# Pooled attention and an MLP on one core: the second MLP product of blocks 4 to 8 by seven products of quarters, copies ahead of remainders, and new priorities

## The chip, the cores and the metric

The kernel runs on one core of one Trainium2 chip. The metric is the device time of one execution in microseconds (us); a run gives the time of several executions, and one execution is also recorded by the hardware profiler. The engines are named as in the profile: PE is TensorE (with PEld, its weight loads), DVE is VectorE, ACT is ScalarE, POOL is GpSimd, and SP is SyncE, which here only issues DMAs.

## The reference

```python
# q, k, v: (4, 8, 1152, 64) float32; w_in (512, 2048) and w_out (2048, 512) float64
q_pool = q.reshape(B, H, S // 2, 2, D).mean(axis=3)              # 576 queries per head
scores = np.matmul(q_pool, k.transpose(0, 1, 3, 2)) / np.sqrt(D)
scores = scores - np.max(scores, axis=-1, keepdims=True)
attn = np.exp(scores)
attn = attn / (np.sum(attn, axis=-1, keepdims=True) + 1e-09)
x = np.matmul(attn, v).transpose(0, 2, 1, 3).reshape(2304, 512)  # 4 batches of 576 tokens
h = x @ w_in
out = np.maximum(0.01 * h, h) @ w_out
```

There are 32 heads (4 batches of 8), each with 576 pooled queries and 1152 keys, and then a two-layer MLP on 2304 tokens.

## The kernel before

**Two pieces for one number.** A float32 operand is split into a high part, rounded to the fast matmul format (`F32R`), and a remainder, also in that format. A product is then three matmuls: high x high, high x remainder, remainder x high. The functions whose names end in `_hi` make the copies, those in `_lo` the remainders (value minus high part).

**Attention.** A head (`hd`) loads its keys and queries, adds pairs of queries (`q_sum`), transposes both on PE (`k_tr`, `q_tr`) into a PSUM bank, and splits them. The keys sit in the bank as two halves of 64 partitions; `k_hi` copies half 0 or 1 on ACT (64 x 512 elements), and `k_lo` subtracts on DVE. For the queries `q_hi` copies each half twice on ACT (64 x 288 elements), and `q_lo` makes the remainder on DVE. The two halves are interleaved in the same tile. Then follow the maxima of the scores (`qk` on PE, `vmax` on DVE), the scores again with the maximum taken off (`qkt`), the exponentials on ACT (`exp`), the sums on POOL (`esum`), the product with the values (`pv`), and the norm. The result goes to DRAM (`xd`), one tile per batch.

**Weights.** In the course of the attention `w_in` and `w_out` are loaded, turned from float64 into float32 and split. The pieces of `w_in` go to DRAM (`wd`) and come back for each block (`ws_load`, 16 tiles of 512 KB); those of `w_out` stay in SBUF (`wo[0..15]`, 128 rows of `w_out` each).

**MLP.** There are 9 blocks of 256 tokens (`i`). A block loads its input (`x_load`) into the only buffer of `xb`, splits it (`x_hi`, `x_lo`), and makes 16 row tiles (`f`) of the hidden layer with `l1`: 12 matmuls of 128 x 128 on 256 columns each. Two of them fill a PSUM bank; `post` applies the leaky ReLU on ACT, copies the high part on DVE or ACT, and makes the remainder on POOL, into a buffer `gg` that is kept until `l2` has read it. `l2` makes the output of 128 tokens (`j`) over 8 row tiles (`hf`), three matmuls of 512 columns per tile; `o_evac` copies the first half of the sum and adds the second on DVE, and `o_out` stores.

A block needs the batches that hold its tokens, so the first blocks run among the heads and the others behind them.

**The order.** Nothing is ordered by the engines themselves: each works through its queue, and waits in it. A planner in the kernel (`Scheduler`) writes the queues. It holds a list of steps, each with a priority, an estimated cost on the engines that could take it, the steps it depends on and the buffers it takes; it goes forward in its own estimated time, and of the steps that can start next takes the one with the smallest priority and the engine on which it would end first. `SHIFT` is a table of numbers added to the priorities, by kind of step and stage. SP's DMA issues are planned in the same way.

Of the kernel before, what the change touches and what calls it, by code (L numbers as in the profile page):

```python
# [9 lines left out]
F32 = mybir.dt.float32  # L10
# [28 lines left out]
PEEK = 0.0  # L39


SHIFT = {
    "esum": (-3.5, 24.75, 81.75, 0, 1.0),
    "exp": (36.25, 13.25, 0, -27.25, 12.75),
    "k_dup": (-5.25, -3.5, 4.5, 0, 8.5),
    "k_hi": (24.5, 16.0, -5.0, -100.0, -3.25),
    "k_lo": (-2.75, -27.0, 0.25, 51.5, -41.0),
    "k_tr": (38.25, 8.5, 23.25, -37.75, 20.0),
    "l1": (-4.75, -21.5),
    "l2": (-19.0, 1.25, 10.0),  # L50
    "load_k": (-73.75, -7.25, -10.0, 2.75, 15.25),
    "load_q": (-16.25, -4.0, 16.5, -12.0),
    "load_v": (0.5, 17.75, 10.0, 3.0, -8.0),
    "m_cp": (20.5, 1.0, 9.5, -10.5, 4.75),
    "m_dma": (-16.25, -44.0, -15.75, 30.25, 27.25),
    "m_side": (146.0, -20.25, 3.25, 12.25, 4.5),
    "m_tr": (-27.25, 0, -0.5, 0, 3.25),
    "norm": (-0.5, 25.0, 28.0, -2.25, 5.75),
    "o_evac": (0, -0.5, 8.0),
    "o_out": (-15.25, 1.0, 11.0),  # L60
    "post0": (9.0, -21.5),
    "post1": (-14.0, -12.5, -14.0),
# [12 lines left out]
    "r_mm": (0, -8.25, -7.75, -6.0, 18.0),
    "r_row": (51.0, -6.5, -20.5, -0.75),
    "r_wide": (1.0, 2.0, 35.5, 1.0, -7.75),
    "scale": (2.75, 0, -8.0, 0, -15.5),
    "vmax": (-16.75, -9.5, 13.0, -138.75, 36.5),
    "vneg": (1.0, 0, 2.0, 4.5),  # L80
    "w_f320": (-1.0, -3.0, -18.75, -38.5),
    "w_f321": (7.0, 127.25, 23.75, -39.75),
    "w_f322": (0, -8.0, 12.5, 44.25),
    "w_hi": (-7.5, 0, -1.25, 7.25),
    "w_lo": (119.75, -10.0, -9.0, -19.75),
    "w_load": (-15.0, 2.25, 18.75, 2.5),
# [30 lines left out]
class Scheduler:  # L117
# [76 lines left out]
    def start(self, s, e, at, pending):  # L194
# [20 lines left out]
        if s.lat:  # L215
            end = self.dma = max(self.dma, at + 1.2) + s.lat
            end += 1.2
# [21 lines left out]
def tile_pooled_attention_moe(  # L239
# [37 lines left out]
    def f32(t):  # L277
        return t.bitcast(F32)
# [31 lines left out]
    }  # L310

    banks = ps.tile([128, 8, 512], F32, name="banks")

    def new(tag, slot, dtype=None):
# [3 lines left out]
        _, shape, dt, _ = spec[tag]  # L318
# [6 lines left out]
        t = sb.tile(spec[own][1], dt, tag=f"{own}{i}", name=own)[:shape[0], :n]  # L325
# [7 lines left out]
    kbs = [sb.tile([128, S], F32R, name=f"kb{j}") for j in range(2)]  # L333
    qzs = sb.tile([128, 5 * 64], F32R, name="qzs")
    qls = [sb.tile([128, NQ * 128], F32R, name=f"ql{j}") for j in range(4)]
# [289 lines left out]
    xx, lps, gf, gg, po, acc = {}, {}, {}, {}, {}, {}  # L625

    def x_load(i, e, s):
        xx[i] = t = new("xb", s)
        n0 = 0
        while n0 < NB:  # L630
            b, o = divmod(i * NB + n0, SP)
# [5 lines left out]
    def x_hi(i, e):  # L637
        copy(e, xx[i][:, 0], f32(xx[i][:, 1]))
# [249 lines left out]
```

## Time and profile before

| what | value |
|---|---|
| median of 3 runs | 935.19 us (934.62 to 939.8) |
| the profiled execution, its own time | 937.15 us |
| its span, first to last instruction | 935.3 us |
| mean granted TensorE clock | 0.944 |
| PE busy | 897.0 us, 96% |
| DVE, ACT, POOL busy | 405.2, 416.1, 502.5 us |

A row of the groups by line reads: line, engine, operation, what is written <- what is read, shapes, count | busy time in total, mean ns of one | the engine's idle time just before, and what ended it. Busy times of PE come from modelled ends of pipelined matmuls; the distance between two starts is the better measure of what a matmul costs.

### The profile page before, as it was taken

The numbers are of one execution on the slowest core, as the hardware profiler recorded it, in microseconds if no ns is written. First come the engines' busy times: TensorE is split into PE (matmuls) and PEld (weight loads), VectorE is DVE, ScalarE is ACT, GpSimd is POOL, SyncE is SP. The second block draws the span as 40 slices with busy tenths as digits, with TensorE's granted clock in tenths as the row PEclk, the third lists the DMA queues.
The fourth block names the chain that finished last, engine by engine and source line by source line (L and its number), as shares of the span: only waits on it lengthen the run. The fifth ranks groups of instructions, "written<-read, shape, count | busy, mean of one in ns | idle before, by whom it ended". The sixth has DMA issues, their size and how long they took to land.

```text
span 935.3 us, 16304 instructions
## 1 busy us (share of the span) xinstructions
PE 897.0 (96%) x6048; PEld 724.4 (77%) x6048; DVE 405.2 (43%) x857; ACT 416.1 (44%) x842; POOL 502.5 (54%) x390
## 2 busy tenths in 40 slices
PE   5999999999899999999999999999999999999998
PEld 3776766677677777877777777787989898989986
DVE  6677887766665544554455544401101011111110
ACT  4677787666556554655665554433111111111110
POOL 2475778867668755766666666657222323232320
PEclk9799999999999999999999999999999999999999
DMA  6389877666656653542454444244658576666630
GB/s 169 100 241 268 246 214 209 182 185 208 204 160 164 194 155 101 162 139 74 144 160 122 123 119 123 66 124 130 226 173 271 189 241 218 204 206 202 221 127 23
DMA packets 113263, 158.66 MB, mean 170 GB/s; under 512 B 21633, under 2 KB 80161, under 8 KB 113185
## 3 DMA queue, kind: packets, MB, share of 16 engines
q1 hardware_dynamic: 113184, 157.64, 56.7%
q8 instruction: 47, 0.77, 0.4%
q14 instruction: 32, 0.25, 0.1%
HBM read 130.02 MB, written 17.90 MB: 158 GB/s over the span
## 4 chain that ended last, share of the span: by engine, by line
PE 73%; ACT 9%; DMA 6%; DVE 6%; issue 4%; SPq 1%; POOL 1%; ACTq 0%; DVEq 0%; POOLq 0%
PE banks L656 20%; PE banks L523 9%; PE banks L472 9%; PE banks L679 7%; PE banks L505 7%; PE banks L680 7%; PE banks L678 7%; PE banks L506 6%; ACT qh L435 3%; ACT ka L281 2%; DVE ka L386 2%; ACT e L510 2%; DMA rt<-rs 2%; DVE ql L439 1%; DMA ws<-wd 1%
## 5 line engine op out<-in xcount | busy, mean ns | idle before, releaser
L510 ACT ACTIVATE e<-banks 128x576 f32<-128x576 f32 x288 | 186.4, 651 | 195.5 <-PE banks L506 184.6
L515 POOL TENSOR_TENSOR sm<-sm,e 128x576 f32<-128x576 f32 x168 | 241.9, 1440 | 53.5 <-ACT e L510 47.5
L475 DVE TENSOR_REDUCE stat<-banks 128x1 f32<-128x384 f32 (+1 forms) x448 | 218.1, 535 | 84.7 <-PE banks L472 80.8
L656 PE MATMUL banks<-xb,ws 128*128 128x256 f32 x1728 | 235.1, 283 | 2.8 <-DMA ws<-wd 1.7
L656 PEld LDWEIGHTS banks<-xb,ws 128*128 128x128 f32 x1728 | 225.0, 189 | 10.3 <-DMA ws<-wd 1.9
L505 PE MATMUL banks<-qh,ka 128*128 128x288 f32 x576 | 170.4, 311 | 6.4 <-ACT e L510 5.9
L506 PE MATMUL banks<-ql,kb 128*128 128x288 f32 x576 | 161.9, 296 | 0.0
L523 PE MATMUL banks<-e,vv 128*64 128x288 f32 x1152 | 159.3, 424 | 0.0
L505 PEld LDWEIGHTS banks<-qh,ka 128*128 128x128 f32 x576 | 109.3, 190 | 33.2 <-ACT e L510 15.1
L472 PE MATMUL banks<-ka,qh 128*128 128x384 f32 x384 | 119.8, 373 | 15.2 <-DVE stat L475 7.0
L664 ACT ACTIVATE g<-banks 128x512 f32<-128x512 f32 x72 | 43.1, 599 | 192.0 <-PE banks L656 191.4
L523 PEld LDWEIGHTS banks<-e,vv 128*64 128x64 f32 x1152 | 78.3, 139 | 64.3 <-issue 16.2
L669 POOL TENSOR_TENSOR gg<-g,gg 128x512 fp32r<-128x512 f32 x50 | 64.4, 1289 | 88.4 <-DVE gg L281 87.3
L506 PEld LDWEIGHTS banks<-ql,kb 128*128 128x128 f32 x576 | 109.4, 190 | 2.4 <-DMA ql<-ms 0.3
L472 PEld LDWEIGHTS banks<-ka,qh 128*128 128x128 f32 x384 | 68.6, 194 | 34.5 <-DVE stat L475 16.9
L515 POOL TENSOR_TENSOR sm<-e 128x576 f32<-128x576 f32 x32 | 46.9, 1465 | 90.0 <-ACT e L510 90.0
L678 PE MATMUL banks<-wo,gg 128*128 128x512 f32 x200 | 79.5, 398 | 0.0
L679 PE MATMUL banks<-wo,gg 128*128 128x512 f32 x200 | 78.9, 395 | 0.0
L680 PE MATMUL banks<-wo,gg 128*128 128x512 f32 x200 | 78.7, 394 | 0.0
L669 POOL TENSOR_TENSOR ka<-g,ka 128x512 fp32r<-128x512 f32 x22 | 28.4, 1291 | 81.5 <-DVE ka L281 81.5
L281 DVE CAST gg<-g 128x512 fp32r<-128x512 f32 x32 | 15.9, 497 | 123.9 <-ACT g L664 123.9
L439 DVE SCALAR_TENSOR_TENSOR ql<-banks,qh 64x288 fp32r<-64x288 f32 x64 | 29.1, 454 | 83.5 <-ACT qh L435 83.1
(66 smaller groups left out, 946.1 us busy)
## 6 DMA issues: line engine op xcount, KB each, us to landing
ws<-wd SPq DMA_DIRECT2D x144, 512.0 KB, 4.6
kn<-in_k_dram SPq DMA_DIRECT2D x32, 288.0 KB, 5.0
qn<-in_q_dram SPq DMA_DIRECT2D x32, 288.0 KB, 4.1
vv<-in_v_dram SPq DMA_DIRECT2D x32, 288.0 KB, 4.7
kb<-ka SPq DMA_DIRECT2D x64, 128.0 KB, 2.9
raw<-in_moe_w_in_dram SPq DMA_DIRECT2D x16, 512.0 KB, 4.5
wd<-ws SPq DMA_DIRECT2D x16, 512.0 KB, 5.8
raw<-in_moe_w_out_dram SPq DMA_DIRECT2D x16, 512.0 KB, 5.5
```

The source lines that it names most:

```text
L472: nc.tensor.matmul(p, lhsT=lhsT, rhs=ka[hd][:, k0:k0 + w], start=(j == 0), stop=(j == 128 // n - 1))
L475: nc.vector.tensor_reduce(out=mx[hd][:, i, c:c + 1], in_=mps.pop((hd, i, c)), axis=AX.X, op=ALU.max)
L505: nc.tensor.matmul(p[:, hf, :HW], lhsT=ka[hd][:, ks], rhs=qh[hd][:, c], start=True, stop=False)
L506: nc.tensor.matmul(p[:, hf, :HW], lhsT=kb[hd][:, ks], rhs=ql[hd][:, c], start=False, stop=True)
L510: nc.scalar.activation(out=ex[hd, t], in_=sps.pop((hd, t))[:, :, :HW], func=AF.Exp)
L515: ENG[e].tensor_tensor(out=sm[hd], in0=ex[hd, 0] if t == 1 else sm[hd], in1=ex[hd, t], op=ALU.add)
L523: nc.tensor.matmul(p[64 * hf:64 * hf + 64, :HW], lhsT=vv[hd][:, t, :], rhs=ex[hd, t][:, hf], start=(t == 0), stop=(t == KT - 1),)
L656: nc.tensor.matmul(p, lhsT=wst[i, f][:, a, c, :], rhs=xx[i][:, x, c, :], start=(n == 0), stop=(n == 3 * KC - 1))
L669: ENG[e].tensor_tensor(out=t[:, 1], in0=gf.pop((i, fp)), in1=f32(t[:, 0]), op=ALU.subtract)
L678: nc.tensor.matmul(p, lhsT=gh, rhs=wo[f][:, 0], start=(f == hf * FH), stop=False)
L679: nc.tensor.matmul(p, lhsT=gh, rhs=wo[f][:, 1], start=False, stop=False)
L680: nc.tensor.matmul(p, lhsT=gl, rhs=wo[f][:, 0], start=False, stop=(f == hf * FH + FH - 1))
```

## The change

In blocks 0 to 3 (`i < FAST`) the MLP stays as it is. In blocks 4 to 8:

- The second product is taken as a product of 2 x 2 quarters: the tokens in two halves of 128, the hidden rows in two halves (row tile `p` and row tile `p + 8`), and the output columns in two halves of 256. In place of eight products of quarters there are seven, of sums and differences of quarters (Winograd's form), each again as three matmuls.
- The sums of the quarters of `w_out` are made once, for each of 8 pairs of row tiles: `w_sum`, then `w_top` (high part, on ACT) and `w_rest` (remainder). One of the four sums overwrites columns of `wo[p]`, so it waits for block 3's use of them. The buffers are those of the attention, after its last head.
- The hidden layer comes in another order (tiles `p + 8` and `p` together); `g_act` applies the leaky ReLU, `g_mix` makes four sums and differences of 128 columns, `g_hi` and `g_lo` the two pieces of all seven.
- `l2s` runs the seven products for one `p`: 21 matmuls of 256 columns into seven halves of four PSUM banks. For the last `p` it goes bank by bank. `o_mix` adds the seven results on DVE (one copy, seven additions), and `o_mix_out` stores.
- `x_load` gets a second buffer, from two buffers of the attention.

In all heads `k_lo` of either half now comes after `k_hi` of both halves, and `q_lo` after all four `q_hi`. The planner's estimate for DMAs changes (300 KB per us in place of 250, and started 0.45 us behind the issue), and the table `SHIFT` is new throughout.

```diff
+FAST = 4
+DEEP = 4
+LAG = 3.5
 SHIFT = {
-    "esum": (-3.5, 24.75, 81.75, 0, 1.0),
-    "exp": (36.25, 13.25, 0, -27.25, 12.75),
+    "esum": (-3.5, 20.75, 83.5, -27.75, -12.25),
+    "exp": (27.75, 25.75, -8.25, -9, 17.25),
...
-            end = self.dma = max(self.dma, at + 1.2) + s.lat
+            end = self.dma = max(self.dma, end + 0.45) + s.lat
...
-    tags["ml"] = [(early, 0, slots("bank", (6,), (3,))), (tail, 0, slots("bank", (0,), (1,), (2,), (3,), (4,), (7,)))]
-    tags["gg"].append((tail, 0, slots("ka", *[(i,) for i in range(spec["ka"][0])])))
+    tags["ml"] = [(early, 0, slots("bank", (6,), (3,))), (tail, 0, slots("bank", (0,), (1,), (2,), (3,), (4,), (5,), (7,)))]
+    end = NHD - 1
+    tags["gg"].append((("k_tr", end, 0), 0, slots("ka", (0,), (1,))))
+    tags["gg"].append((("k_dup", end), 0, slots("kb", (0,))))
+    tags["xb"].append((("k_tr", end, 0), 0, slots("ka", (2, 3))))
+    tags["wf"] = [(("k_tr", end, 0), 0, slots("ka", (0,))), (("k_dup", end), 0, slots("kb", (0,)))]
...
+    S1, S2, S3, S4, A12, A22, A11, A21 = range(8)
+    PRODUCTS = ((0, 0, A11), (0, 1, A12), (1, 0, S2), (1, 1, S1), (2, 0, S3), (2, 1, A22), (3, 0, S4))
+    def w_sum(p, part, e, i=None):
...
+        tt = ENG[e].tensor_tensor
+        if part == 0:
+            for n, a, b in ((2, b22, b12), (0, b12, b11)):
+                tt(out=t[:, n:n + 2], in0=a, in1=b, op=ALU.subtract)
+                tt(out=t[:, n], in0=t[:, n], in1=t[:, n + 1], op=ALU.add)
+        else:
+            for n, a, b, op in ((1, b22, 0, ALU.subtract), (3, b21, 1, ALU.subtract)):
+                tt(out=t[:, n], in0=a[:, 0], in1=t[:, b], op=op)
+                tt(out=t[:, n], in0=t[:, n], in1=a[:, 1], op=ALU.add)
...
+    def w_rest(p, n, e):
+        t = wt2[p, n]
+        ENG[e].tensor_tensor(out=t[:, 1], in0=wf[p][:, n], in1=f32(t[:, 0]), op=ALU.subtract)
+    def g_act(i, p, e, s):
+        fs_[i, p] = new("gf", s, F32)
+        src = lps.pop((i, p)).rearrange("p y n -> p (y n)")
+        dst = fs_[i, p][:, A12:].rearrange("p a n -> p (a n)")
+        nc.scalar.activation(out=dst, in_=src, func=AF.Prelu, alpha=0.01)
+    def g_mix(i, p, e):
+        t = fs_[i, p]
+        for o, a, b, op in ((S1, A21, A22, ALU.add), (S3, A11, A21, ALU.subtract), (S2, S1, A11, ALU.subtract), (S4, A12, S2, ALU.subtract)):
+            ENG[e].tensor_tensor(out=t[:, o], in0=t[:, a], in1=t[:, b], op=op)
+    def g_hi(i, p, e, s):
+        gh[i, p] = new("gs", s)
+        copy(e, gh[i, p].rearrange("p a n -> p (a n)"), fs_[i, p][:, :7].rearrange("p a n -> p (a n)"))
+    def g_lo(i, p, e, s):
+        gl[i, p] = new("gs", s)
+        ENG[e].tensor_tensor(out=gl[i, p], in0=fs_.pop((i, p))[:, :7], in1=f32(gh[i, p]), op=ALU.subtract)
+    def l2s(i, p, b, e, *got):
...
+        ws = (b11, b21, t2, t1, t3, t4, b22)
+        for (bank, half, a), w in zip(PRODUCTS, ws):
+            if b is not None and bank != b:
+                continue
+            o = pk[i, bank][:, 256 * half:256 * half + 256]
+            for n, (g, x) in enumerate(((gh, 0), (gh, 1), (gl, 0))):
+                nc.tensor.matmul(
+                    o, lhsT=g[i, p][:, a], rhs=w[:, x], start=(p == 0 and n == 0 and half == 0),
...
-                step(k_lo, hd, x, prio=pr + 0.1 * g, eng={"DVE": dve(n, psum=True)}, deps=[("k_hi", hd, x)])
+                step(k_lo, hd, x, prio=pr + 0.1 * g, eng={"DVE": dve(n, psum=True)}, deps=[("k_hi", hd, x), None if g else ("k_hi", hd, 1)])
...
-            step(q_lo, hd, x, prio=pr + 0.5, eng={"DVE": dve(HW, psum=True)}, deps=[("q_hi", hd, x, x)])
+            step(q_lo, hd, x, prio=pr + 0.5, eng={"DVE": dve(HW, psum=True)}, deps=[("q_hi", hd, 1, y) for y in range(2)])
...
+    for p in range(FH):
+        pr = 500 + p
+        last = [("l2s", NBLK - 1, p, 3 if p == FH - 1 else None)]
+        pools = {"POOL": 2 * (gp(512) + gp(256)), "DVE": 2 * (dve(512) + dve(256))}
+        step(w_sum, p, 0, prio=pr, eng=pools, lock=True, deps=[("w_lo", NF + p), ("w_lo", NF + FH + p)], takes=[("wf", [("w_rest", p, n) for n in range(4)])])
+        step(w_sum, p, 1, prio=pr, eng={"POOL": 4 * gp(256), "DVE": 4 * dve(256)}, lock=True, deps=[("w_sum", p, 0)])
+        for n in range(4):
+            deps = [("w_sum", p, n % 2)] + ([("w_sum", p, 1)] + [("l2", FAST - 1, 0, 1, x) for x in (p,)] if n == 0 else [])
+            takes = [("w2" if p == 0 and n == 1 else "w1", last)] if n and not (p == 0 and n == 2) else []
+            step(w_top, p, n, prio=pr, eng={"ACT": act(256)}, deps=deps + ([("w_top", 0, 1)] if p == 0 and n == 2 else []), takes=takes)
+            step(w_rest, p, n, prio=pr, eng={"POOL": gp(256), "DVE": dve(256)}, lock=True, deps=[("w_top", p, n)])
...
+                last = [("l2s", i, fp, x) for x in (range(4) if fp == FH - 1 else (None,))]
+                step(g_act, i, fp, prio=POST, eng={"ACT": act(512, True)}, deps=[("l1", i, f, 2)], takes=[("gg", [("g_lo", i, fp)], 2)])
+                step(g_mix, i, fp, prio=POST, eng={"DVE": 4 * dve(128), "POOL": 4 * gp(128)}, lock=True, deps=[("g_act", i, fp)])
+                step(g_hi, i, fp, prio=POST, eng={"ACT": act(7 * 128)}, deps=[("g_mix", i, fp)], takes=[("gg", last, 1)])
+                step(g_lo, i, fp, prio=POST, eng={"POOL": gp(7 * 128), "DVE": dve(7 * 128)}, lock=True, deps=[("g_hi", i, fp)], takes=[("gg", last)])
```

## Rows read from the trace of the kernel before

**Rows 1.** The page: span, and busy time of PE.

```profile
span 935.3 us, 16304 instructions
PE 897.0 (96%) x6048; PEld 724.4 (77%) x6048; DVE 405.2 (43%) x857; ACT 416.1 (44%) x842; POOL 502.5 (54%) x390
```

**Rows 2.** Windows: length, then busy us of each engine, clock, DMA share, GB/s.

```profile
0.00:100.00 100.00, 87.01 (x549) 62.62 (x551) 72.41 (x153) 63.97 (x136) 52.33 (x51) 0.91 0.70 197
100.00:640.00 540.00, 519.59 (x3671) 403.42 (x3667) 299.88 (x636) 310.98 (x637) 364.58 (x279) 0.95 0.55 155
...
656.00:932.00 276.00, 274.40 (x1729) 246.57 (x1725) 31.90 (x67) 35.61 (x60) 73.49 (x53) 0.95 0.59 194
```

**Rows 3.** Groups by line: a weight load (whole run), PE from 656 to 932.

```profile
L656 PEld LDWEIGHTS banks<-xb,ws 128*128 128x128 f32 x1728 | 225.0, 189 | 10.3 <-DMA ws<-wd 1.9 <-ACT raw L281 1.5 <-issue 0.9
...
L656 PE MATMUL banks<-xb,ws 128*128 128x256 f32 x1128 | 145.3, 282 | 1.1 <-ACT raw L281 1.1
L679 PE MATMUL banks<-wo,gg 128*128 128x512 f32 x111 | 43.9, 395 | 0.0
...
L679 PE MATMUL banks<-wo,ka 128*128 128x512 f32 x88 | 34.8, 395 | 0.0
```

**Rows 4.** Timeline of PE, the last block: start, length, line, count.

```profile
905.56 3.03 PE L656 MATMUL banks<-xb,ws 128*128 128x256 f32 x24
908.43 0.39 PE L678 MATMUL banks<-wo,ka 128*128 128x512 f32 x1
...
931.12 0.39 PE L680 MATMUL banks<-wo,ka 128*128 128x512 f32 x1
```

**Rows 5.** Groups of PE from 908.35 to 931.3; three of each pattern.

```profile
L679 PE MATMUL banks<-wo,gg 128*128 128x512 f32 x20 | 7.9, 394 | 0.0
...
L679 PE MATMUL banks<-wo,ka 128*128 128x512 f32 x13 | 5.1, 394 | 0.0
```

**Rows 6.** Groups by line: casts (30 to 640, 656 to 932), then elementwise work.

```profile
L281 DVE CAST gg<-g 128x512 fp32r<-128x512 f32 x7 | 5.2, 747 | 22.1 <-ACT g L664 22.1
...
L281 DVE CAST gg<-g 128x512 fp32r<-128x512 f32 x25 | 10.7, 427 | 101.8 <-ACT g L664 101.8
L688 DVE TENSOR_TENSOR raw<-banks,raw 128x512 f32<-128x512 f32 x13 | 8.9, 688 | 34.6 <-PE banks L680 18.9 <-issue 15.7
...
L386 DVE TENSOR_TENSOR ka<-banks,ka 64x128 fp32r<-64x128 f32 x32 | 9.1, 284 | 1.0
...
L439 DVE SCALAR_TENSOR_TENSOR ql<-banks,qh 64x288 fp32r<-64x288 f32 x64 | 29.1, 454 | 83.5 <-ACT qh L435 83.1
...
L669 POOL TENSOR_TENSOR gg<-g,gg 128x512 fp32r<-128x512 f32 x25 | 32.3, 1291 | 84.9 <-DVE gg L281 84.9
...
L567 POOL TENSOR_TENSOR x<-x,rs 128x288 f32<-128x288 f32 x1 | 0.8, 810 | 1.1 <-DMA rs<-rd 1.1
...
L664 ACT ACTIVATE g<-banks 128x512 f32<-128x512 f32 x47 | 28.1, 599 | 185.6 <-PE banks L656 185.6
...
L281 ACT CAST xb<-xb 128x1024 fp32r<-128x1024 f32 x1 | 1.0, 1040 | 0.0
...
L281 ACT CAST ka<-banks 64x512 fp32r<-64x512 f32 x64 | 37.1, 579 | 15.6 <-PE banks L370 10.3 <-DVE ka L386 4.6
```

**Rows 7.** DMA issues: an input tile, KB each, us from issue to landing.

```profile
xb<-xd SPq DMA_DIRECT2D x6, 512.0 KB, 6.2
```

**Rows 8.** Timeline of the end: the last DVE addition.

```profile
931.60 0.69 DVE L688 TENSOR_TENSOR raw<-banks,raw 128x512 f32<-128x512 f32 x1 [4.85 <-PE banks L680]
```

**Rows 9.** Waits of ACT, whole run: us in total, times, longest.

```profile
ACT qh L435 <- DVE ql L439: 18.2, 32, 0.9
...
ACT ka L281 <- DVE ka L386: 4.6, 10, 0.6
```

**Rows 10.** Waits of PE from 100 to 640 us.

```profile
PE banks L505 <- ACT e L510: 5.9, 12, 0.6
...
PE banks L472 <- DVE ka L386: 4.0, 6, 1.1
...
PE banks L472 <- ACT qh L435: 0.9, 1, 0.9
```

More of the change, by code (lines that the diff above doesn't have):

```diff
@@ L324, in new @@
             n *= x
-        t = sb.tile(spec[own][1], dt, tag=f"{own}{i}", name=own)[:shape[0], :n]
+        t = sb.tile(FIXED[own] if own in FIXED else spec[own][1], dt, tag=f"{own}{i}", name=own)
+        if len(t.shape) > 2:
+            old = "abc"[:len(t.shape) - 1]
+            t = t.rearrange(f"p {' '.join(old)} -> p ({' '.join(old)})")
+        t = t[:shape[0], :n]
         names = "abcd"[:len(shape) - 1]
@@ L627, in x_load @@
     def x_load(i, e, s):
-        xx[i] = t = new("xb", s)
+        if len(s) == 1:
+            t = new("xb", s)
+            xx[i] = t[:, 0], t[:, 1]
+        else:
+            xx[i] = [new("x1b", (y,)) for y in s]
         n0 = 0
@@ new lines, in w_top @@
+    def w_top(p, n, e, i=None):
+        if n == 0:
+            wt2[p, n] = wo[p][:, :, 256:]
+        elif i is not None and i[0][0] == "kb":
+            t = new("w2", i)
+            wt2[p, n], wt2[p, n + 1] = t[:, 0:2], t[:, 2:4]
+        elif i is not None:
+            wt2[p, n] = new("w1", i)
+        copy(e, wt2[p, n][:, 0], wf[p][:, n])
+    def w_rest(p, n, e):
[6 more added lines that the diff above has]
+        nc.scalar.activation(out=dst, in_=src, func=AF.Prelu, alpha=0.01)
@@ new lines, in l2s @@
+    def l2s(i, p, b, e, *got):
+        if got:
+            for n, s in enumerate(got):
+                pk[i, n] = new("ml", s)
+        t1, t2, t3, t4 = (wt2[p, n] for n in range(4))
+        b11, b21, b22 = wo[p][:, :, :256], wo[p + FH][:, :, :256], wo[p + FH][:, :, 256:]
+        ws = (b11, b21, t2, t1, t3, t4, b22)
[6 more added lines that the diff above has]
+                    o, lhsT=g[i, p][:, a], rhs=w[:, x], start=(p == 0 and n == 0 and half == 0),
+                    stop=(p == FH - 1 and n == 2),
+                    skip_group_check=True,
+                )
@@ new lines, in o_mix @@
+    def o_mix(i, n, e, *got):
+        if got:
+            oc[i] = [new("raw", x) for x in got]
+        c11, c12, c21, c22 = (oc[i][j][:, 256 * x:256 * x + 256] for j in range(2) for x in range(2))
+        half = [pk[i, b][:, 256 * x:256 * x + 256] for b in range(4) for x in range(2)]
+        p1, p2, p6, p5, p7, p4, p3, _ = half
+        if n == 0:
+            return copy(e, c12, p1)
+        o, a, b, op = (
+            (c11, c12, p2, ALU.add), (c12, c12, p6, ALU.add), (c22, c12, p5, ALU.add), (c21, c12, p7, ALU.add),
+            (c21, c21, p4, ALU.add), (c12, c22, p3, ALU.add), (c22, c22, p7, ALU.add),
+        )[n - 1]
+        nc.vector.tensor_tensor(out=o, in0=a, in1=b, op=op)
@@ L671, in l2, with o_mix_out @@
+    def o_mix_out(i, j, e):
+        r0 = i * NB + j * 128
+        nc.sync.dma_start(out=out[r0:r0 + 128, :], in_=oc[i][j])
     def l2(i, hf, j, f, e, s=None):
@@ L817, in tile_pooled_attention_moe @@
     for i in range(NBLK):
         pr = 1000 + 10 * i
[L819 removed]
+        step(x_load, i, prio=-100, **sp(1 + (i * NB // SP != (i * NB + NB - 1) // SP), 0.524e6), deps=[("x_out", hd) for hd in needs(i)] + [("x_load", i - 1) if i else None], takes=[("xb", [("l1", i, FH - 1 if i >= FAST else NF - 1, 2)])])
```

202 lines of the change are left out of this document (133 added, 69 removed).

## The prediction

> **What bounds the kernel now.** I read the page first: TensorE (PE) is busy 897.0 of 935.3 us [rows 1], so little can be won by filling its gaps, and the question is how much of its work the change takes out. A busy PE is not yet a PE at its own pace, because the ends of pipelined matmuls are modelled, so I went on to the windows by stage. They show three stages [rows 2]: the first 100 us with 13 us of PE idle, the attention of the 32 heads from 100 to 640 us with 20.4 us idle in 540, and from 656 us on the MLP alone, with 1.6 us idle in 276. The reader should see that VectorE (DVE) and ScalarE (ACT) have 32 and 36 us of work in that last stage, and GpSimd (POOL) 73: there PE sets the time alone.
>
> Is it dense there? The groups of PE by line count 1128 matmuls of 256 columns (first product) and 3 x 111 + 3 x 88 = 597 of 512 columns (second product) [rows 3]. Their pitch I take from starts in the timeline, not from the durations of 0.28 and 0.39 us, which overlap. Twenty-four of 256 columns run from 905.56 to 908.43: 0.1196 us each. Ninety-nine of 512 columns start between 908.43 and 931.12, 98 steps: 0.2315 us each [rows 4, 5]. Then 1128 x 0.1196 + 597 x 0.2315 = 134.9 + 138.2 = 273.1 us, against 275.3 from 656 to the end of PE. So a microsecond taken out of the MLP's columns is a microsecond of the kernel, as long as PE is fed.
>
> **The products of quarters.** Per block of 256 tokens the second product is now 16 x 2 x 3 = 96 matmuls of 512 columns: 96 x 0.2315 = 22.2 us. The change makes it 8 pairs x 7 products x 3 = 168 of 256 columns: 168 x 0.1196 = 20.1 us. It saves 2.13 us a block, 10.7 us in blocks 4 to 8. A narrow pitch read wrong by 0.002 us would be 840 x 0.002 = 1.7 us: I take 10.7, bounds 9.0 and 12.4. Not 1/8 of 22.2 (2.8), because each matmul carries a fixed part: two narrow ones cost 0.239 where one wide costs 0.2315. A narrow matmul has its own weight load, but so has every one of the first product [rows 3], which is the row with the same shape in and out.
>
> **What feeds it.** For each pair of rows the activation now goes through ACT (0.60, as before), four sums of 128 elements, an ACT copy of 896 and a subtraction of 896. From the 128-element and 512-element rows of DVE, 0.284 and 0.688 us, an element costs about 1.05 ns, so the sums take 4 x 0.28 and the subtraction 1.09; the ACT copy of 896 is just under that of 1024, 1.04, say 0.93 [rows 6]. The chain is 0.60 + 1.14 + 0.93 + 1.09 = 3.8 us plus hand-offs. Meanwhile PE has a pair of first product (24 x 0.12 = 2.9 us) and a pair of quarters (21 x 0.12 = 2.5) per 5.4 us and runs up to four pairs ahead: hidden. If that cover were gone, each of 40 pairs would show some 4 us.
>
> The weight sums are new work: per pair of weight rows two of 512 and ten of 256 elements, each near 0.69 and 0.42 us on DVE (0.454 for 288 [rows 6]), 5.6 us, 45 us for all eight, plus 32 ACT copies. They need buffers that come free with the last head, so they fall from some 640 us on, under block 3. The columns that are overwritten in place must wait for block 3's first half of the second product, and there are two buffers for the differences: from the third pair on they follow that half. Behind it PE still has block 3's second half (48 x 0.2315 = 11.1) and four pairs of block 4 (11.5 us), and each later pair is wanted 5.4 us after the one before, at about the 5.6 us that one costs. So this is nearly hidden, without much to spare. At the seam the pairs of block 4 also wait for block 3's activation buffers, which come free only in its last 11 us: PE may wait for the 3.8 us chain once. Bounds 0 and 3.8, I take 1.0; the case in which the sums are really late is a rival below.
>
> Input tiles get a second buffer and weight tiles come in another order, the same 512 KB each. An input tile takes 6.2 us to land [rows 7]; today the second product trailing behind the first hides it, since idle PE in the last stage is 1.6 us [rows 2] for six blocks, and the four pairs of quarters that trail in future (4 x 2.5 = 10 us) hide it as well, even before the second buffer helps: 0. Without cover it would be some 6 us and a copy in each of five blocks. The tail grows: the last matmul starts at 931.12, one DVE addition of 0.69 follows, then the store [rows 4, 8]. Afterwards four additions of 256 remain behind the last two banks, 4 x 0.42 = 1.7 less 0.4 under the last three matmuls, 1.3 for 0.69, and two stores come together instead of one: 0.6 to 1.5, I take 1.0.
>
> **The copies and the priorities.** Today the ACT copy of the second half of the queries waits for DVE's subtraction on the first: 18.2 us over the 32 heads, and 4.6 for the keys [rows 9]. With all copies ahead ACT no longer has these 22.8 us of waiting. The chain of one head gets no shorter: copies (0.58 for keys) and subtractions still run after each other [rows 6, 9], and the first subtraction even starts one copy later. What is won is that the exponentials queued on ACT behind the copies come sooner. From 100 to 640 PE waits for ACT 5.9 + 0.9 = 6.8 us [rows 10]; I take two thirds, 4.5 us. Bounds: nothing gained, or the whole idle of that stage, 20.4 us [rows 2]. The new priorities move every engine's order and every DMA issue in SP's queue, where an issue that waits holds all behind it; the trace of before cannot price that. It can lose as well: a key subtraction 0.58 us later in 32 heads is 18.6 us if every one met a waiting PE, but only 4.0 us of PE's waits go to it now [rows 10]. I take 0 for the priorities by themselves, bounds of 8 either way.
>
> **The sum.** Profiled execution 937.15 - 10.7 + 1.0 (seam) + 1.0 (tail) - 4.5 = 924.0. That execution is 1.96 above the median of the runs, so on the median's scale 922.0 us.
>
> **Rivals.**
> The elementwise pair is late (ends slower). DVE and POOL share something: the same 512-element cast takes 0.43 us in the MLP stage and 0.75 from 30 to 640, where POOL works two thirds of the time [rows 6, 2]. If POOL gets the sums, at 1.29 us for 512 and 0.81 for 288 [rows 6], so 2.15 ns an element and 0.74 for 256, 0.46 for 128 and 2.1 for 896, then the weights cost 80 us, a block's activations 8 x (4 x 0.46 + 2.1) = 32, block 3's own work 13: 125 us from 656, done at 781. The last pair of block 4 is wanted at about 753: 656, and 117 wide and 168 narrow matmuls left of blocks 0 to 3 (597 - 480, 1128 - 960; 47 us), and 11.5 for four pairs of block 4, and seven pairs of 5.4. Some 28 us late, against 10.7 saved: 922 + 28 - 1 = 949. From about 18 us of lateness on, the kernel is slower. Against it: DVE has 32 us of work in 276 [rows 2] and each step may go to either engine. Chance 0.08.
>
> The Trainium skill speaks for this rival: its page "SBUF — State Buffer", section "Who interferes with whom", says that a VectorE instruction with two SBUF inputs and a GpSimd instruction that reads SBUF exclude each other for a whole instruction. All the new sums are of that kind. The cast's two durations agree that there is a conflict; that it holds for sums with two inputs no row here shows. By that rule DVE's and POOL's work adds up: 45 for the weights, 24 for block 4 (8 x 2.23 for its pairs, 3 for its last sums and 3 for its input) and 17 for block 3 as today, 86 us in the 97 from 656 to 753, so it would still fit if the sums lie on DVE.
>
> The gain is given back: the new order costs some 8 us or the seam its full 3.8: 930 to 936, no measurable change. For it: 20.4 us of idle in attention are waits of many kinds that any order moves. Chance 0.16.
>
> The new order wins more: half of both idles, 13 + 20.4 [rows 2], is 17 us in place of 4.5: 909. Chance 0.12.
>
> Narrow matmuls run at the pace of their weight loads, 0.189 us [rows 3]: 840 x 0.189 = 159 us where 111 were, 970. The first product's 0.1196 beside the same loads speaks against it. Chance 0.02.
>
> **Chances and range.** My forecast has 0.62, with a range of its own of 914 to 929. A measurement of this kernel can tell about 0.5% (4.7 us) from no change. Faster: 0.62 + 0.12 and little of the third rival, 0.76. Same: 0.15. Slower: the first and the last rival, 0.09. The range reaches up into the given-back case and down to the order that wins more: 909 to 933.
>
> **What would show it.** Right: 840 matmuls of 256 columns at a pitch of 0.12 on the new line in place of 480 wide ones, about 20 us a block; a block of the MLP near 43 us; ACT's waits for the query subtraction gone; from the end of attention to PE's last matmul some 10 us less than 275. Wrong: PE waiting in block 4 for a weight remainder or an activation remainder, PE idle in 100 to 640 above 25 us, or a last attention matmul later than 656.

## The result, and the profile after

The changed kernel takes 912.7 us (median of 4 runs, 910.57 to 915.53) against 934.9 us before (median of 4): 22.2 us by the medians, and as a ratio, which leaves disturbed runs out, 0.9735, 95% interval 0.9703 to 0.9767. It is faster. The forecast was 922.0 us and faster; the range 909 to 933 holds the result, but the forecast's own range, 914 to 929, does not. The profiled execution took 910.57 us.

The page, first its span and busy times [rows 1], then the windows that answer to [rows 2] (length, busy us of PE, PEld, DVE, ACT, POOL, then clock, DMA share, GB/s):

```profile
span 908.8 us, 17344 instructions
...
PE 873.0 (96%) x6408; PEld 731.1 (80%) x6408; DVE 528.6 (58%) x1135; ACT 464.0 (51%) x911; POOL 454.0 (50%) x351
```

```profile
0.00:100.00 100.00, 84.31 (x545) 60.95 (x547) 77.92 (x156) 64.04 (x134) 53.40 (x52) 0.97 0.69 199
100.00:640.00 540.00, 526.50 (x3792) 415.67 (x3790) 305.00 (x647) 320.65 (x652) 376.56 (x287) 1.00 0.57 159
...
656.00:932.00 276.00, 246.22 (x1977) 241.15 (x1975) 143.57 (x328) 77.89 (x122) 17.24 (x9) 0.99 0.56 181
```

The share of PE is the same 96%; its work is less, and in 100 to 640 us it is idle 13.5 us where it was 20.4. DVE does in the last stage 144 us where it did 32, POOL 17 where it did 73: the sums went to DVE.

Where the stages end is seen in the timeline of PE: the last matmul of the attention, and the start of the last matmuls of all. First after, then a second trace of the kernel before (run E9, taken beside E10 to E12):

```profile
641.29 0.41 PE L571 MATMUL banks<-e,ones 128*32 128x288 f32 x2
...
903.08 0.52 PE L784 MATMUL banks<-wo,gg 128*128 128x256 f32 x3
```

```profile
657.62 0.41 PE L534 MATMUL banks<-e,ones 128*32 128x288 f32 x2
...
933.13 0.39 PE L680 MATMUL banks<-wo,ka 128*128 128x512 f32 x1
```

The last of the three matmuls after starts at 903.32, so the MLP alone took 262.0 us, against 275.5 in either trace of before (655.66 to 931.12 in the first). The attention ended 16.3 us sooner than in E9 and 14.4 sooner than in the first trace. From PE's last start to the end of the span it is 5.5 us in place of 4.2. So -14.4 - 13.4 + 1.3 = -26.5 us of span, 935.3 to 908.8. The filler that stands among the heads (MLP matmuls) is the same work in both: 648 of 256 columns and 243 of 512 after, 600 and 267 before, 133 us each.

**The products.** The chain that ended last shows the last stage, from 702 us on, as a strict alternation (start, length, line, count), with no step for anything but PE until the tail:

```profile
709.59 2.82 PE banks L703 x24
712.41 2.48 PE banks L784 x21
714.89 2.85 PE banks L703 x24
717.74 2.47 PE banks L784 x21
```

Twenty-one matmuls of quarters in 2.48 us are 0.1181 us each, 168 of them 19.8 us a block. That is a little under the 0.1196 that I took from [rows 4], where the hand-over to the wide matmuls was counted in.

**The attention.** The 14 us need another measure, since PE counts as busy wherever a matmul's modelled end covers the next start. I took the distance between neighbouring starts in the timeline of PE, less count x pitch (0.119 us for 256 columns, 0.2315 for 512, 0.1325 for 288, 0.1725 for 384, 0.1335 for the float32 ones of the values), and put what is left to the matmul that comes next. This is my arithmetic on the timeline, not a view; it is good to a few us, and better for the difference of two rows than for a sum (the float32 matmuls of the values start 0.249 us a pair apart in E9 and after, less than twice 0.1335). From 100 to 630 us it gives 49.2 us of gaps in E9 and 30.4 after, and nearly all of the difference lies ahead of two kinds of matmul: the scores (they wait for a PSUM pair that an exponential on ACT must release), 24.7 to 16.7, and the product for the maxima (it waits for a bank that DVE's maximum releases, and for DVE's key remainders), 17.2 to 8.6. PE's waits from 100 to 632 us agree for ACT, where [rows 10] has 5.9 us:

```profile
PE banks L542 <- ACT e L547: 0.8, 3, 0.4
```

The experiments stand in one table, by this measure:

| kernel | ratio to before (95%) | last attention matmul, us | gaps 100 to 630 | ahead of scores | ahead of maxima product |
|---|---|---|---|---|---|
| E9 before again | - | 657.6 | 49.2 | 24.7 | 17.2 |
| E2 copies alone | 1.0003 (0.9977 to 1.0028) | 656.0 | 44.6 | 20.4 | 21.0 |
| E5 copies, queues kept | 0.9982 (0.9960 to 1.0004) | 650.8 | 43.2 | 16.8 | 16.9 |
| E3 priorities and estimate alone | 1.0119 (1.0091 to 1.0147) | 656.5 | 46.5 | 25.9 | 13.7 |
| E10 DMA estimate alone | 1.0146 (1.0101 to 1.0192) | 656.5 | 47.8 | 27.3 | 14.9 |
| E1 quarters alone | 0.9887 (0.9848 to 0.9927) | 664.9 | 53.9 | 25.9 | 18.7 |
| E4 all but quarters | 0.9918 (0.9895 to 0.9940) | 641.0 | 29.8 | 15.8 | 7.1 |
| after | 0.9735 (0.9703 to 0.9767) | 641.3 | 30.4 | 16.7 | 8.6 |
| E6 after, remainders between, queues kept | 0.9932 (0.9908 to 0.9957) | 660.2 | 46.0 | 26.8 | 13.9 |
| E7 after without copies ahead | 0.9875 (0.9828 to 0.9923) | 660.1 | 48.8 | 28.1 | 13.0 |
| E11 after, old DMA estimate | 0.9860 (0.9831 to 0.9888) | 652.6 | 39.4 | 21.0 | 14.0 |
| E8 no quarters, old MLP priorities | 0.9963 (0.9943 to 0.9983) | 643.8 | 32.8 | 15.5 | 9.3 |
| E12 quarters from block 3 | 0.9811 (0.9773 to 0.9849) | 646.4 | 35.4 | 16.8 | 9.7 |

Each experiment's ratio is to runs of before on the same chip, so a difference of two rows carries both intervals. The ends of the attention compare only with the same filler ahead of them: E2 has 4.5 us less than before, E10 8.4 less, E1 1.5 less, E11 6.4 less than after. Runs of one kernel spread by 2 to 10 us (E4: 930.42 to 932.21, E2: 935.16 to 944.81, and its trace is the slowest of them), so the ratios, from several runs, decide on small differences, and the gaps say where.

### The profile page after: what moved, and what is told of

Same layout as the page of the kernel before. It is cut to its first block, busy times and chain, and to the rows that moved or that the text cites. A ratio compares the mean times of both kernels' runs of the same rounds, so it can differ in the third digit from the quotient of the medians.

```text
span 908.8 us, 17344 instructions
## 1 busy us (share of the span) xinstructions
PE 873.0 (96%) x6408; PEld 731.1 (80%) x6408; DVE 528.6 (58%) x1135; ACT 464.0 (51%) x911; POOL 454.0 (50%) x351
## 4 chain that ended last, share of the span: by engine, by line
PE 77%; DMA 9%; ACT 3%; POOL 3%; SPq 3%; issue 3%; DVE 2%; ACTq 0%; POOLq 0%; DVEq 0%
PE banks L703 21%; PE banks L560 11%; PE banks L784 11%; PE banks L509 8%; PE banks L542 7%; PE banks L543 6%; PE banks L816 3%; PE banks L818 3%; PE banks L817 3%; DMA raw<-in_moe_w_in_dram 3%; DMA ws<-wd 2%; POOL sm L552 2%; SPq L585 2%; PE banks L571 2%; PE banks L407 1%
## 5 line engine op out<-in xcount | busy, mean ns | idle before, releaser
L703 PE MATMUL banks<-xb,ws 128*128 128x256 f32 x1152 | 160.9, 283 | 0.8 <-DMA ws<-wd 0.7
L703 PEld LDWEIGHTS banks<-xb,ws 128*128 128x128 f32 x1152 | 151.1, 189 | 2.6 <-DMA ws<-wd 0.9
L542 PEld LDWEIGHTS banks<-qh,ka 128*128 128x128 f32 x576 | 109.2, 190 | 28.4 <-issue 12.4
L423 DVE TENSOR_TENSOR ka<-banks,ka 64x512 fp32r<-64x512 f32 (+1 forms) x96 | 53.1, 554 | 104.4 <-ACT ka L294 89.0
L703 PE MATMUL banks<-ka,ws 128*128 128x256 f32 x576 | 71.9, 280 | 1.4 <-DMA ws<-wd 1.4
L703 PEld LDWEIGHTS banks<-ka,ws 128*128 128x128 f32 x576 | 69.8, 188 | 2.0 <-DMA ws<-wd 1.8
L784 PE MATMUL banks<-wo,gg 128*128 128x256 f32 x312 | 59.9, 282 | 0.0
L472 ACT ACTIVATE qh<-banks 64x288 fp32r<-64x288 f32 x128 | 51.7, 404 | 3.5 <-PE banks L465 2.1
L294 ACT CAST ka<-banks 64x512 fp32r<-64x512 f32 (+1 forms) x96 | 45.0, 470 | 13.7 <-PE banks L407 12.6
L457 POOL TENSOR_TENSOR qs<-qn 96x384 f32<-96x384 f32 x32 | 32.0, 1000 | 34.2 <-PE banks L465 22.0
L784 PEld LDWEIGHTS banks<-wo,gg 128*128 128x128 f32 x312 | 46.9, 188 | 0.1
```

The lines of the kernel that those rows point to most:

```text
L294: ENG[e].copy(out=out, in_=in_) if e == "ACT" else ENG[e].tensor_copy(out=out, in_=in_)
L423: nc.vector.tensor_tensor(out=d[64 - o:128 - o], in0=src, in1=f32(d[o:o + 64]), op=ALU.subtract)
L472: nc.scalar.activation(out=q_half(qh[hd], x)[64 * y:64 * y + 64], in_=src, func=AF.Copy, scale=QSCALE)
L542: nc.tensor.matmul(p[:, hf, :HW], lhsT=ka[hd][:, ks], rhs=qh[hd][:, c], start=True, stop=False)
L703: nc.tensor.matmul(p, lhsT=wst[i, f][:, a, c, :], rhs=xx[i][x][:, c, :], start=(n == 0), stop=(n == 3 * KC - 1))
L784: nc.tensor.matmul(o, lhsT=g[i, p][:, a], rhs=w[:, x], start=(p == 0 and n == 0 and half == 0), stop=(p == FH - 1 and n == 2), skip_group_ ...
```

## The experiments

Each run's order is made anew by the kernel's planner, but in E5 and E6 ("queues kept") the planner's result is recorded and only the named steps change places. All of them compute the whole output.

**E1, quarters alone.** After, with the old lines for copies and DMA, and the old rows of `SHIFT` for the old kinds.

```diff
-                step(k_lo, hd, x, prio=pr + 0.1 * g, eng={"DVE": dve(n, psum=True)}, deps=[("k_hi", hd, x), None if g else ("k_hi", hd, 1)])
+                step(k_lo, hd, x, prio=pr + 0.1 * g, eng={"DVE": dve(n, psum=True)}, deps=[("k_hi", hd, x)])
...
-            end = self.dma = max(self.dma, end + 0.45) + s.lat
+            end = self.dma = max(self.dma, at + 1.2) + s.lat
...
-    "exp": (27.75, 25.75, -8.25, -9, 17.25),
+    "exp": (36.25, 13.25, 0, -27.25, 12.75),
```

> Before with the products of quarters alone: copies, DMA estimate and the old kinds' priorities as before, the new kinds' priorities as after. My theory: the MLP stage, from the last attention matmul to PE's last one, falls by 11 to 13 us from 275, the attention stage (ends at 656 us before) stays within 2 us, and the kernel gains 9 to 12 us. Rival (the gain of the attention stage comes with the quarters, since other buffers and banks come free): the attention stage ends at about 642 as in after, and the kernel gains 20 or more. Rival (the pair of DVE and POOL is late without the new priorities): PE waits in block 4, gain under 6 us.

Measured: 0.9887, so 10.6 us faster (6.8 to 14.3). The attention gained nothing (gaps 53.9), PE waited in the last stage for neither sums nor remainders. My theory held for the kernel's gain and for the products: the MLP alone took 262.3 us, 13.2 less than in before. It did not hold for the attention, which ends at 664.9 in this trace and not within 2 us of 656; the trace is the slowest of the four runs.

**E2, copies alone.** Before, with the two `deps` of the change:

```diff
...
-            step(q_lo, hd, x, prio=pr + 0.5, eng={"DVE": dve(HW, psum=True)}, deps=[("q_hi", hd, x, x)])
+            step(q_lo, hd, x, prio=pr + 0.5, eng={"DVE": dve(HW, psum=True)}, deps=[("q_hi", hd, 1, y) for y in range(2)])
```

> Before with only the order of copies and remainders changed, priorities old. My theory: ACT's waits for the subtractions (18.2 and 4.6 us) go, PE's waits for ACT fall from 6.8 to some 2 us, the kernel gains 3 to 6 us, all of it before 656 us. Rival (the order was never on PE's path and its value comes only with new priorities): within 2 us of before, though ACT's waits are gone. Rival (the later first subtraction holds up the next head): 2 to 10 us slower.

Measured: 1.0003, nothing. ACT's waits for the subtractions are gone, PE's waits for ACT fell from 6.8 to 3.9 us (2.5 and 1.4), but in this trace PE's waits for the key remainders rose from 4.0 to 6.0 us and gaps ahead of the maxima product from 17 to 21. My theory failed; the first rival held.

**E3, priorities and DMA estimate alone.** Before, with the new `SHIFT` of the old kinds and the new estimate:

```diff
-            end = self.dma = max(self.dma, at + 1.2) + s.lat
+            end = self.dma = max(self.dma, end + 0.45) + s.lat
...
-    "exp": (36.25, 13.25, 0, -27.25, 12.75),
+    "exp": (27.75, 25.75, -8.25, -9, 17.25),
```

> Before with only the new priorities of the old kinds and the new DMA estimate; no quarters, copies in the old order. My theory as on record: within 3 us of before. Rival (the attention stage's 14 us come from the new order of the queues): 8 to 14 us faster, attention ending 8 to 14 us before 656. Rival (the granted clock, 0.95 in the one trace and 1.00 in the other, makes the 14 us): no gain here if the clock is the same as in before's run, and the clock differs from run to run without the kernel.

Measured: 1.0119, 11 us slower. The attention ended where it did before (656.5), and the MLP alone took 286.4 us, 11 more (below, E8 and E10). Neither my "within 3 us" nor the rival with a gain held.

**E4, everything but the quarters.** E3 with the two edits of `deps` that E2 has (its diff is E2's and E3's together).

> After without the products of quarters: copies ahead, new priorities of the old kinds, new DMA estimate, second product of all blocks as before. My theory: 9 to 13 us slower than after, so 10 to 13 us faster than before, with attention ending near 642 us and an MLP stage of some 275 us. Rival (the new priorities only pay with the quarters): attention ends at 650 or later, gain over before under 6 us.

Measured: 0.9918, 7.7 us faster; attention ends at 641.0 with gaps of 29.8 us, as in after. E3 and E4 differ in the copies alone: there they are worth 19 us, in E2 nothing. But from E4 to after it is 17 us, more than the 12 of the products less 1.3 of tail. PE's waits in the last stage of E4 show why (waiting, releaser: us in total, times, longest; "issue" is a wait that the profile cannot name):

```profile
PE banks L656 <- issue: 6.6, 5, 1.6
```

Five waits, one at the first matmuls of each block, where the input tile and its pieces have just come: for one block the load was issued at 667.21 us, the copy of the tile ran from 673.80 to 674.49, and PE went on at 674.60.

**E5, the queues of before with the copies ahead.** The planner's order is recorded, and before a remainder is emitted the copies of both halves are; in the queues only two ACT entries change places, and ACT's wait goes.

```diff
-        s.run(e, *got)
+        self.emit.append((s.key, partial(s.run, e, *got)))
...
+        todo = dict(self.emit)
+        for key, go in self.emit:
+            if key[0] in ("q_lo", "k_lo") and key[2] < 2:
+                hi = key[0][0] + "_hi"
+                for x in range(2):
+                    for y in range(2) if hi == "q_hi" else (None,):
+                        k = (hi, key[1], x) if y is None else (hi, key[1], x, y)
+                        if k in todo:
+                            todo.pop(k)()
+            if key in todo:
+                todo.pop(key)()
```

> Before with the queues of all engines kept as planned, and only the copies emitted ahead of the remainders: five ACT and DVE entries change places, what goes is ACT's wait of 18.2 + 4.6 us. My theory as on record: 3 to 6 us faster than before. Rival (copies and priorities only pay together, since the freed ACT time must be used by another order): within 2 us of before. Rival (it pays, and the planner gave it back in the run with copies alone, where the whole order moved): 5 us or more faster, with the gaps of PE ahead of the scores (46 us in 100 to 640) well under 40.

Measured: 0.9982, 1.7 us (from 3.7 faster to 0.4 slower): less than my 3 to 6, and what the first rival said. (Its one trace ends the attention 4.8 and 6.8 us sooner than the two of before; ten runs do not bear that out.) PE's waits from 100 to 640 us show what became of it, first E9, then E5:

```profile
PE banks L505 <- ACT e L510: 7.2, 13, 0.7
PE banks L472 <- DVE stat L475: 6.7, 8, 2.1
```

```profile
PE banks L484 <- DVE stat L487: 9.3, 10, 2.2
...
PE banks L517 <- ACT e L522: 0.9, 4, 0.3
```

The waits for ACT's exponentials went from 7.2 to 0.9 us, and the waits for DVE's maxima rose from 6.7 to 9.3. In this order DVE is late next.

**E6, the queues of after with the remainders between.** The reverse: the first half's remainder is emitted ahead of the second half's copies. Some 30 DVE entries move, nothing on another engine.

```diff
+            if key[0] in ("q_hi", "k_hi") and key[2] < 2:
+                lo = (key[0][0] + "_lo", key[1], 1 - key[2])
+                hi = [(key[0], key[1], 1 - key[2], y) for y in range(2)] if key[0] == "q_hi" else [(key[0], key[1], 1 - key[2])]
+                if lo in todo and not any(k in todo for k in hi):
+                    todo.pop(lo)()
```

> After with the queues of all engines as planned, and only the remainders of the first half emitted ahead of the copies of the second half, as before: ACT waits for DVE again. Theory A (the new order needs ACT free): 10 us or more slower than after, PE's gaps from 100 to 640 back from 30 to over 40 us. Theory B (the gain is the new order of the queues itself): under 5 us slower than after, gaps near 33 us.

Measured: 0.9932 against after's 0.9735, 18.5 us slower, with gaps of 46.0 us: theory A. One head in the timeline of ACT, first after, then E6 (start, length, idle before, releaser):

```profile
436.76 0.65 ACT L547 ACTIVATE e<-banks 128x576 f32<-128x576 f32 x1 [1.04 <-PE banks L543]
437.42 0.82 ACT L472 ACTIVATE qh<-banks 64x288 fp32r<-64x288 f32 x2
438.25 1.17 ACT L294 CAST ka<-banks 64x512 fp32r<-64x512 f32 x2
439.44 0.82 ACT L472 ACTIVATE qh<-banks 64x288 fp32r<-64x288 f32 x2
440.29 0.41 ACT L577 ACTIVATE rs<-banks 128x288 f32<-128x288 f32 x1
440.60 0.65 ACT L547 ACTIVATE e<-banks 128x576 f32<-128x576 f32 x1
```

```profile
449.31 0.65 ACT L557 ACTIVATE e<-banks 128x576 f32<-128x576 f32 x1 [1.04 <-PE banks L553]
449.97 0.82 ACT L482 ACTIVATE qh<-banks 64x288 fp32r<-64x288 f32 x2
450.82 0.58 ACT L304 CAST ka<-banks 64x512 fp32r<-64x512 f32 x1
452.15 0.58 ACT L304 CAST ka<-banks 64x512 fp32r<-64x512 f32 x1 [0.75 <-DVE ka L433]
452.75 0.82 ACT L482 ACTIVATE qh<-banks 64x288 fp32r<-64x288 f32 x2
453.60 0.41 ACT L587 ACTIVATE rs<-banks 128x288 f32<-128x288 f32 x1
453.90 0.65 ACT L557 ACTIVATE e<-banks 128x576 f32<-128x576 f32 x1
```

And the matmul of E6 that waits for it, in PE's timeline:

```profile
454.60 0.40 PE L552 MATMUL banks<-qh,ka 128*128 128x288 f32 x1 [0.50 <-ACT e L557]
```

The new order puts all copies of a head into one block between two exponentials: 3.84 us from one to the next. With the wait it is 4.59, and PE stands 0.50 us for the second exponential; in after the scores follow the product of the values without a gap. Over the attention ACT's waits of this kind in E6 are:

```profile
ACT ka L304 <- DVE ka L433: 27.1, 32, 2.1
...
ACT qh L482 <- DVE ql L486: 13.0, 25, 0.9
```

40 us where after has none: in the new order the wait that the copies remove is almost twice as long as in the old one, 22.8 us [rows 9], and lies where PE waits for it. From 100 to 640 us PE's waits for the exponentials are, in E6,

```profile
PE banks L552 <- ACT e L557: 9.5, 19, 1.0
```

where after has 0.8. ACT's queue is the same in E6 and after, entry for entry: the wait comes from what the program emits first, and a copy that is emitted behind a subtraction waits for it. The two share a tile and a PSUM bank; which of them makes the wait no run separates.

**E7, after without the copies ahead, planned anew.** The `deps` of `k_lo` and `q_lo` as before (E2's diff the other way round).

> After with the old dependency of the remainders, everything planned again: quarters and new priorities, copies in the old order. Theory A (copies carry the gain): 10 to 20 us slower than after, like the run of priorities alone against the run without quarters. Theory B (priorities are fitted to one plan, and any edit of the steps loses it): also slower, but then the frozen queues with the remainders between lose less than half as much.

Measured: 0.9875, 13 us slower than after. Theory A held by its number. E6 lost at least as much as this run, so B as I had worded it did not.

**E8, no quarters, new attention priorities, old MLP priorities** (the edit against E4).

```diff
...
     "exp": (27.75, 25.75, -8.25, -9, 17.25),
...
-    "l1": (-4.75, -27.5, -7.5),
-    "l2": (-19, 22.25, 14),
+    "l1": (-4.75, -21.5),
+    "l2": (-19.0, 1.25, 10.0),
...
-    "x_load": (3.25, -11.75, 0.25),
+    "x_load": (4.75, 0, -2.75),
```

> Without quarters: copies ahead, new priorities for attention and weights, old priorities for the MLP's kinds, new DMA estimate. Theory (the run without quarters lost 8 us in the MLP stage because the new MLP priorities count on the second input buffer): attention ends near 640 us with the same filler, MLP stage 275 to 277 us, total 7 to 10 us below the run without quarters, 14 to 18 us below before. Rival (the MLP's priorities also place the filler in the attention): attention ends 5 us or more later, total no better than the run without quarters.

Measured: 0.9963 (0.9943 to 0.9983), slower than E4. The attention kept its gain (ends at 643.8, gaps 32.8), but the five waits at block starts stayed, 6.5 us. My theory on the MLP's priorities fell.

**E9, before again**, for its trace.

> The kernel before, unchanged, on the chip of the experiments, for its trace there: granted clock 0.99 in place of 0.944. Theory (the clock has no part in the result): attention ends at 654 to 660 us with the same filler, gaps of PE from 100 to 630 between 44 and 50 us, span near 935. Rival (the clock makes part of the 14 us of attention): the product with the values at 412 ns in place of 424, attention ends 4 us or more earlier than 655.9.

Measured: 939.16 us, with the numbers above; at a mean granted clock of 0.989 the attention ended 2 us later, not sooner, than at 0.944. So the slower clock of the first trace does not make the 14 us. But the clock has a part in each single trace. In the first it is a steady 0.95 [rows 2], and each pair of matmuls of the values takes 0.258 us from start to start in place of 0.249: some 5 us over 576 pairs, by my estimate. E9 has the full clock, but falls to half of it for two stretches from 100 to 630 us, and after for one (windows as above, first E9, then after):

```profile
124.00:128.00 4.00, 1.88 (x13) 1.39 (x10) 4.00 (x5) 1.43 (x4) 2.24 (x2) 1.00 0.85 229
128.00:135.00 7.00, 6.25 (x24) 5.64 (x25) 4.75 (x11) 5.55 (x13) 4.54 (x4) 0.51 0.81 254
...
244.10:247.60 3.50, 3.50 (x12) 3.22 (x12) 2.06 (x6) 1.16 (x2) 1.42 (x2) 0.51 0.89 275
```

```profile
138.30:141.70 3.40, 3.40 (x14) 2.84 (x13) 2.11 (x6) 2.14 (x4) 0.77 (x1) 0.50 0.62 181
```

Just before each fall PE had waited: 1.88 us busy of 4 in the first row. At half clock the matmuls of 288 columns start 0.24 us apart in place of 0.1325, so E9's stretches hold some 5 us of its gaps and after's 1.7: of the 18.8 us between the two some 3.5 are clock, by my estimate. The result itself is not clock: at mean clocks of 0.991 to 0.994 the 21 runs of before on record took 934.3 to 942.9 us, and the four of after 910.6 to 915.5.

**E10, the DMA estimate alone.** Before, with

```diff
-            end = self.dma = max(self.dma, at + 1.2) + s.lat
+            end = self.dma = max(self.dma, end + 0.45) + s.lat
...
-        return dict(eng={"SP": 0.45 * n}, lat=nbytes / 250e3 * max(1.0, 512 / run))
+        return dict(eng={"SP": 0.45 * n}, lat=nbytes / 300e3 * max(1.0, 512 / run))
```

> Before with only the planner's DMA estimate changed. Theory (the hopeful estimate makes the planner put too little work between the load of an input tile and its use, as in the three runs that have it without the second input buffer): five waits of PE of 0.6 to 3 us at the starts of blocks in the MLP stage, 5 to 8 us together, where before has none. The attention may go either way by 5 us, since its order is planned anew. Rival: no such waits, so they come from the new priorities.

Measured: 1.0146, 13.7 us slower. PE's waits in the last stage:

```profile
PE banks L656 <- issue: 7.6, 5, 2.2
```

Theory held: the estimate makes these waits, which E3, E4 and E8 have with it. They are about half of the loss; the rest lies in the attention, which ends no sooner though 8.4 us less MLP work stands in it. In before the planner kept enough second product behind to cover an input tile of 6.2 us [rows 7]; believing in an earlier arrival it keeps less. In after they are gone; that the second input buffer does it is argued from the code, not tried alone.

**E11, after with the old estimate** (E10's diff the other way round).

> After with the old DMA estimate. Theory (any edit of the plan's inputs moves the order away from the one that the priorities were fitted to): 4 to 15 us slower than after, all in the attention stage, MLP stage unchanged at some 262 us. Rival (the attention gain needs the copies and the priorities alone): within 3 us of after.

Measured: 0.9860, 12 us slower than after, all up to the end of the attention (gaps 39.4). The MLP alone took 267.0 us and not 262, but with 6.4 us more work left for it, and its only wait is 0.9 us. So the new priorities need the new estimate as they need the copies: they are positions in one particular order.

**E12, quarters from block 3 on.**

```diff
-FAST = 4
+FAST = 3
```

> After with the products of quarters from block 3 on. If nothing else moved, 2.2 us more saved. Theory (the weight sums of 45 us fall right behind the attention, and block 3's quarters are wanted at once): PE waits 5 us or more for them near 650 us, so no faster than after, 3 to 10 us slower. Rival (the first product of block 4 fills in): 2 us faster than after, the best of all.

Measured: 0.9811 (0.9773 to 0.9849), some 7 us slower than after. PE waits in the last stage, from 683 to 710 us, for the pieces of the weight sums:

```profile
PE banks L784 <- DVE e L751: 3.1, 2, 1.7
PE banks L784 <- DVE qh L751: 1.7, 1, 1.7
PE banks L784 <- ACT qh L294: 1.6, 1, 1.6
PE banks L784 <- ACT e L294: 0.8, 1, 0.8
```

Theory held, if not for the place (650 us). Block 3 is the cover of the weight sums; without it they cost 7.2 us of waits. The attention, planned anew, also ended 5 us later in this trace. No run beats after.

## Why the prediction came out as it did

**The products, right.** 10.7 us forecast, bounds 9.0 to 12.4. By pitch it is 480 x 0.2315 - 840 x 0.1181 = 11.9 us, and E1 shows 10.6 with the tail. The MLP stage fell by 13.4 us. Mean distances of starts over the whole stage account for the 1.5 us beyond the pitch: the wide matmuls of before stand 0.2325 us apart there, not 0.2315 (0.5 us on 480), and the 1080 of the first product go from 0.1194 to 0.1186 us (0.9 us), why, I have not resolved. PE's waits are alike, 1.1 us before and 1.4 after.

**What feeds them, right.** These rows of DVE and ACT in the last stage answer to the durations worked out from [rows 6], 0.28 us for 128 elements (0.32 here), 0.42 for 256, 0.93 and 1.09 for 896. The weight sums began at 618.7 us, sooner than the 640 of the prediction.

```profile
L762 DVE TENSOR_TENSOR gg<-gg 128x128 f32<-128x128 f32 x72 | 19.9, 317 | 17.9 <-ACT gg L757 17.3
...
L770 DVE TENSOR_TENSOR gg<-ka,gg 128x896 fp32r<-128x896 f32 x11 | 12.0, 1092 | 9.0 <-ACT gg L294 8.5 <-PE banks L784 0.4
...
L733 DVE TENSOR_TENSOR kb<-kb 128x256 f32<-128x256 f32 x8 | 3.4, 425 | 0.3
```

```profile
L294 ACT CAST gg<-ka 128x896 fp32r<-128x896 f32 x12 | 11.3, 941 | 19.1 <-DVE ka L762 19.1
```

**The seam.** 1.0 us forecast for the activation chain; PE waited once from 632 us on, 1.4 us, and for a weight tile:

```profile
PE banks L703 <- DMA ws<-wd: 1.4, 1, 1.4
```

**The tail**, 1.0 forecast, 1.3 measured: seven additions on DVE, then two stores together.

```profile
902.28 2.97 DVE L803 TENSOR_TENSOR raw<-raw,banks 128x256 f32<-128x256 f32 x7 [4.78 <-ACT raw L294]
...
904.82 0.81 SPq L807 DMA_DIRECT2D out_dram<-raw  x2
```

**The copies and the priorities, wrong in size.** The step that failed is "From 100 to 640 PE waits for ACT 5.9 + 0.9 = 6.8 us; I take two thirds, 4.5 us", and with it "0 for the priorities by themselves". The attention gave 14 us (some of either trace's gain is clock, E9; by the ratios, 24.8 us in all less E1's 10.6, it is 14 too). Two errors lie in that step. First, I sized the gain by what PE's idle time shows, 6.8 us of waits out of 20.4 us, though I had just written that its ends are modelled; by starts the gaps were 46 us in the trace that I had (49 in E9), more than twice the idle time, and 30 of them are left in after. The gain stayed under my bound of 20.4 all the same. Second, I priced the two edits one by one. Alone, in the old queues, the copies gave 1.7 us, and the wait passed on to DVE (E5); alone, the priorities with their estimate left the attention's end where it was and lost 11 us behind it (E3). Together they gave the 14: the new order brings the product for the maxima clear of DVE (17 to 9 us ahead of it) and stacks the copies, which it can afford only when they do not wait for DVE (E6, 18.5 us). The sum 924.0 of the profiled execution so missed by 13.4 us (9.3 on the scale of the medians): 10 in the attention, the rest in the MLP stage.

**The rivals.** "The new order wins more", at 0.12 and 909 us, is what happened, but its number came near by luck: it takes half of the idle in both early stages, 17 us, and PE's idle in the first 100 us went from 13.0 to 15.7 us, in 100 to 640 from 20.4 to 13.5. The late pair did not come: 31 of the 32 weight remainders went to DVE, and block 3 covered them; E12 shows its price where there is no cover. The pace of the weight loads did not bind, 0.1181 us beside loads of 0.188. The given-back gain is what the copies alone show (E2, E5).

**Open.** Which of the new rows of `SHIFT` takes the product for the maxima clear of DVE was not tried, nor the second input buffer by itself, nor copies and priorities with the old estimate and without quarters.

## What to carry to other kernels

Size a possible gain on a pipelined engine by the distance of its starts less count x pitch, not by its idle time: here 20 us of idle stood for 46 us of gaps. Before an ordering edit is priced, ask which engine is late next; one wait removed in an order that has a second one right behind it gives next to nothing, and the same edit can be worth 18 us in an order that was made for it. Where a planner writes the queues, try an edit with the recorded queues as well as with new ones, because every change of an estimate or a dependency is also a new order.

## What the runs showed of the hardware that was not expected

A DVE subtraction of 256 elements with both inputs in SBUF takes 0.42 us, and 2.41 us when it meets a POOL subtraction (timelines of DVE and POOL, after):

```profile
682.08 2.41 DVE L751 TENSOR_TENSOR qh<-kb,qh 128x256 fp32r<-128x256 f32 x1 [2.10 <-ACT qh L294]
...
686.46 0.42 DVE L751 TENSOR_TENSOR vv<-kb,vv 128x256 fp32r<-128x256 f32 x1
```

```profile
681.82 2.39 POOL L683 TENSOR_TENSOR xb<-xb 128x1024 fp32r<-128x1024 f32 x1 [4.70 <-ACT xb L294]
```

POOL began 0.26 us earlier and was done at 684.21, DVE at 684.49: it waited POOL out. That is what the Trainium skill says on its page "SBUF — State Buffer", section "Who interferes with whom", of a VectorE instruction with two SBUF inputs beside a GpSimd instruction that reads SBUF, and which the rows of before could not show. Eleven of the new sums of after began while POOL was at work and took 0.4 to 2.2 us longer than their like; one that began 0.16 us ahead of a POOL subtraction, at 675.55 us, took its 0.42.

The granted clock of the two traces of before differs: a steady 0.95 in one, full with stretches at half in the other (E9), means 0.944 and 0.989. With it the matmuls of the values differ (mean 424 and 412 ns), but the times are alike, 937.15 and 939.16 us.
